# Moving the first head's key bits to ScalarE, making the bit offsets first, and fewer warm products: the start of a hash-attention and Sinkhorn-MoE kernel

## The chip, the cores and the metric

The kernel runs on one core of one Trainium2 chip. The metric is the device time of one execution in microseconds (us), as the median of several. All executions told of here were classed as fast; "clock" is the mean clock granted to TensorE, 1.0 being full. In the profiles PE is TensorE, PEld its weight loads, DVE is VectorE, ACT is ScalarE, POOL is GpSimd and SP is SyncE; a q behind an engine's name is its sequencer, which waits and issues transfers. PSUM is the memory in which this kernel has TensorE's results.

## The reference

```python
# q, k, v: (4, 8, 768, 64); proj: (64, 6)
q_bits = einsum('bhsd,dk->bhsk', q, proj) > 0      # six hash bits for each query, and so for keys
mask   = q_bucket[..., :, None] == k_bucket[..., None, :]
scores = where(mask, q @ k.T / 8, -1e9)
attn_out = softmax(scores) @ v
x = attn_out as (3072, 512)
# then: logits = x @ w_gate, 8 Sinkhorn iterations, 8 experts of relu(x @ w1[e]) @ w2[e], summed
```

## The kernel before

Eight groups of four heads go one after the other through the attention; the experts follow. A query's bits are appended as seven more rows to its 64 values, and a key's likewise, so that one product gives score and mask. `prepare(n)` makes group n ready; for group 1, VectorE transposes k and q, TensorE hashes, VectorE makes the bits (L414 to L417). Group 0 has a routine of its own, because everything waits for it:

```python
def place(name, h, c, copy):            # 32x768 float32 -> float16, all in on-chip memory
    pin(copy(d[name][32*c:32*(c+1), h, :], trs[name][32*h:32*(h+1), c, :]))

def at_once():                          # group 0
    ...
    for name in "kq":
        turn_qk(name, 0)                # VectorE transposes; GpSimd casts the result (t16)
        place(name, 0, 0, nc.scalar.copy)
        hash_twice(name, 0)             # TensorE: hash of the first two heads
        turn_qk(name, 1)
        place(name, 0, 1, nc.scalar.copy)
        ...
        warm_up(9 if name == "q" else 4)
    ...                                 # bits of k: VectorE reads PSUM, then x BIG in place
    move("k", 0)                        # two VectorE copies 7x384, the key bits of head 0
    put("k")
    ...                                 # query bits of head 0: two VectorE operations from PSUM
    ...                                 # query bits of all: one VectorE operation from PSUM
    put("q")
    place("q", 1, 1, nc.vector.tensor_copy)
    move("k", 1)                        # two copies each: bits of head 1
    move("q", 1)
    ...
    cast_v()                            # GpSimd: two casts of v, then six sums for its mean
```

For group 1, VectorE transposes k and q, TensorE hashes, VectorE makes the bits (L414 to L417) and copies those of its head 0 (L431). The bits of its other heads go to a DRAM buffer and come back:

```python
    stack("q", 0)                       # SyncE: two transfers each
    stack("q", 1)
    ...
    put_bits()                          # SyncE: ds <- bt, 96 KB to DRAM
    ...
    get_bits("k", h); get_bits("q", h)  # SyncE: back from DRAM; waits for the write
    ...
    fetch(2, "kq")                      # GpSimd: 2 x 768 KB from DRAM for group 2
```

`pin` keeps an instruction behind the one traced before it on its engine. Without it an instruction goes where the scheduler thinks it is needed.

The softmax here doesn't subtract the row's maximum and nothing guards it: scores larger than these inputs give would overflow.

Of the kernel before, what the change touches and what calls it, by code (L numbers as in the profile page):

```python
# [20 lines left out]
def kernel(  # L21
# [11 lines left out]
    nc = tc.nc  # L33
    B, H, S, D = q.shape
    assert (B, H, S, D) == (4, 8, 768, 64)
    NB = proj.shape[1]
# [10 lines left out]
    HT = S // 2  # L47
# [5 lines left out]
    R = 32  # L53
# [3 lines left out]
    KR = D + NB + 1  # L57
# [4 lines left out]
    def pin(ins):  # L62
        tc.keep_in_program_order(ins)
        return ins
# [3 lines left out]
    proj4 = consts.tile([P, 2, NB], F32)  # L68
# [302 lines left out]
    def prepare(n):  # L371

        d = grp[n] = {}
# [13 lines left out]
        def turn_qk(name, c):  # L387
            i_ap = nat[name, n][:, :, 32 * c:32 * (c + 1)]
            o_ap = trs[name][:, c, :]
            if name == "k":  # L390
                i_ap = i_ap.rearrange("p (m t) d -> p m t d", m=M4)
                o_ap = o_ap.rearrange("p (t m r) -> p m t r", t=KT, m=M4)
            else:
                o_ap = o_ap.rearrange("p (m r) -> p m r", r=R)
            pin(nc.vector.transpose(o_ap, i_ap))
            pin(nc.gpsimd.tensor_copy(t16s[name][:, c, :], trs[name][:, c, :]))

        def stack(name, h):
            for c in range(2):
                pin(nc.sync.dma_start(out=d[name][32 * c:32 * (c + 1), h, :],  # L400
                                         in_=t16s[name][32 * h:32 * (h + 1), c, :]))
# [22 lines left out]
        def get_bits(name, h):  # L424
            pin(nc.sync.dma_start(out=d[name][D:KR, h, :].rearrange("r (j t) -> r j t", j=2),
                                       in_=dss["kq"]["kq".index(name), :, h, 0:NB + 1, :].rearrange("j r t -> r j t")))
# [6 lines left out]
        def cast_v():  # L433
            v32 = wk.tile([P, 2, 3, D], F32, tag="v32", name="v32", bufs=1)
            for i in range(2):
                hs = slice(2 * i, 2 * i + 2)
                pin(nc.gpsimd.tensor_copy(va[:, hs, :, 0:D],
                                          nat["v", n][:, hs, :].rearrange("p h (t d) -> p h t d", d=D)))
            for i in range(2):
                hs = slice(2 * i, 2 * i + 2)  # L440
                pin(nc.gpsimd.tensor_tensor(v32, va[:, hs, 0:3, 0:D], va[:, hs, 3:6, 0:D], op=Alu.add))
                pin(nc.gpsimd.tensor_tensor(v32[:, :, 0], v32[:, :, 0], v32[:, :, 1], op=Alu.add))
                pin(nc.gpsimd.tensor_tensor(vs[:, hs, 0:D], v32[:, :, 0], v32[:, :, 2], op=Alu.add))

        def place(name, h, c, copy):
            pin(copy(d[name][32 * c:32 * (c + 1), h, :], trs[name][32 * h:32 * (h + 1), c, :]))

        def at_once():
            bt = wk.tile([P, 2, S], F16, tag="t16", name="bt0")

            def hash_twice(name, c):
                for g, table in enumerate((pb.rearrange("p c a r -> p c (a r)"), pb1)):
                    for x in range(2):
                        o = 64 * g + 32 * x
                        pin(nc.tensor.matmul(d["pr" + name][o:o + 32, 0, 0:HT], table[:, c, :],
                                             trs[name][:, c, x * HT:(x + 1) * HT], start=(c == 0), stop=(c == 1)))

            def move(name, h):
                for x in range(2):
                    p = 64 * h + 32 * x  # L460
                    pin(nc.vector.tensor_copy(d[name][D:KR, h, x * HT:(x + 1) * HT],
                                              bt[p:p + NB + 1, "kq".index(name), 0:HT]))

            def put(name):
                i = "kq".index(name)
                pin(nc.sync.dma_start(out=dss["kq"][i].rearrange("j h r t -> (j h r) t"), in_=bt[0:64, i, 0:HT]))

            dss["kq"] = scr.tile([2, 2, HG, 8, HT], F16, tag="ds", name="ds")
            for name in "kq":
                d["pr" + name] = sps.tile([P, 2, 512], F32, tag="s", name="pr0")  # L470
                turn_qk(name, 0)
                place(name, 0, 0, nc.scalar.copy)
                hash_twice(name, 0)
                turn_qk(name, 1)
                place(name, 0, 1, nc.scalar.copy)
                if name == "k":
                    place("k", 1, 0, nc.scalar.copy)
                else:
                    place("k", 1, 1, nc.scalar.copy)
                    place("q", 1, 0, nc.scalar.copy)  # L480
                hash_twice(name, 1)
                warm_up(9 if name == "q" else 4)
                for h in range(2, HG if name == "k" else 3):
                    stack(name, h)
            k_, q_ = bt[:, 0, 0:HT], bt[:, 1, 0:HT]
            pin(nc.vector.tensor_scalar(k_, d["prk"][:, 0, 0:HT], 0.0, 0.5, op0=Alu.is_gt, op1=Alu.subtract))
            pin(nc.vector.tensor_scalar(k_, k_, BIG, None, op0=Alu.mult))
            move("k", 0)
            put("k")
            for x in range(2):  # L490
                sl = slice(32 * x, 32 * x + NB + 1)
                pin(nc.vector.tensor_scalar(d["q"][D:KR, 0, x * HT:(x + 1) * HT], d["prq"][sl, 0, 0:HT], 0.0, qoff[sl, 0:1],
                                            op0=Alu.is_gt, op1=Alu.subtract))
            pin(nc.vector.tensor_scalar(q_, d["prq"][:, 0, 0:HT], 0.0, qoff[:, 0:1], op0=Alu.is_gt, op1=Alu.subtract))
            put("q")
            place("q", 1, 1, nc.vector.tensor_copy)
            move("k", 1)
            move("q", 1)
            stack("q", 3)
            for h in range(2, HG):  # L500
                get_bits("k", h)
                get_bits("q", h)
            cast_v()

        if n == 0:
            at_once()
            return
# [177 lines left out]
    fetch(0, "v", nc.sync)  # L685
    fetch(1, "kq", nc.sync)
    pb1 = acc_flat[:, 24 * DD - 2 * R:24 * DD].rearrange("p (c m) -> p c m", c=2)
    nc.vector.memset(pb1, 0.0)
    nc.vector.tensor_copy(pb1[R:2 * R, :, 0:NB], proj4[R:2 * R])
    warm = ops.tile([P, 512], F32, tag="o", name="warm")  # L690

    def warm_up(count):
        for _ in range(count):
            pin(nc.tensor.matmul(warm, tiny, tiny.unsqueeze(1).to_broadcast([P, 4, P]), start=True, stop=True))
# [14 lines left out]
    for u in range(len(units) + 1):  # L709
        if u < len(units):  # L710
            n, h, kt = units[u]
# [239 lines left out]
```

## Time and profile before

| | before |
|---|---|
| median of the first three runs | 766.67 us (766.44 to 767.45) |
| span of the profiled run | 765.1 us |
| TensorE, VectorE, ScalarE, GpSimd busy | 98%, 74%, 67%, 42% |
| first query transpose | 8.94 us |
| first exp, first exp of group 1 | 14.27, 33.94 us |

The first query transpose starts when q has landed from DRAM. It is the time zero of most comparisons below, called T0, because that landing differs from run to run though no edit touches the load. An exp is one ScalarE instruction of the softmax, the exponential of 128x768 scores. The first exp shows when the first scores are ready; the first exp of group 1 (exp 24, counted from 0) shows what is left of a shift when the second group starts.

### The profile page before, as it was taken

The page shows a single profiled execution, that of the slowest core. Times are in us where ns is not written, and L with a number is a line of the kernel's source. Part 1 is how long each engine was busy: PE and PEld are TensorE (multiplying, and loading weights), DVE is VectorE, ACT ScalarE, POOL GpSimd, SP SyncE. Part 2 cuts the span into 40 slices and gives each one's busy share as a digit, 9 for nine tenths or more (in the row PEclk, how much of TensorE's full clock was granted, in tenths as well). Part 3 has the DMA queues.
Part 4 walks back from the last instruction along what each step waited for, and adds up shares of the span by engine and source line. Part 5 has one row for each costly group of instructions (what it writes and reads, how often), then busy time and mean ns, then how long its engine had stood idle before and what let it go on. Part 6 is the DMA issues. An engine that isn't in the chain of part 4 may idle for free.

```text
span 765.1 us, 16738 instructions
## 1 busy us (share of the span) xinstructions
PE 747.5 (98%) x6294; PEld 517.2 (68%) x6294; DVE 567.4 (74%) x1261; ACT 514.0 (67%) x1027; POOL 318.3 (42%) x327
## 2 busy tenths in 40 slices
PE   8999999999999999999999999999999999999997
PEld 3655566566654677777777777777777777777664
DVE  6787666667579777777777777777777777777774
ACT  6986786678655777766666666666666666666661
POOL 6766353449200433443344334433543344324222
PEclk9999999999999999999999999999999999999999
DMA  8779447841030464776477648754964496443335
GB/s 227 203 195 227 126 128 174 175 124 27 2 56 8 83 108 80 125 126 115 90 130 132 112 84 144 121 95 83 171 118 90 91 165 112 84 84 83 84 77 145
DMA packets 41569, 88.08 MB, mean 115 GB/s; under 512 B 7232, under 2 KB 21840, under 8 KB 41488
## 3 DMA queue, kind: packets, MB, share of 16 engines
q0 software_dynamic: 27168, 69.49, 46.9%
q1 hardware_dynamic: 13324, 16.48, 8.2%
q10 hardware_dynamic: 996, 1.05, 0.6%
q8 instruction: 49, 0.80, 0.5%
q14 instruction: 32, 0.26, 0.1%
HBM read 53.05 MB, written 7.08 MB: 79 GB/s over the span
## 4 chain that ended last, share of the span: by engine, by line
PE 84%; DVE 6%; ACT 6%; issue 1%; DMA 1%; SPq 0%; ACTq 0%; DVEq 0%
PE a L829 18%; PE a L250 18%; PE d L829 13%; PE y L250 9%; PE st L570 6%; PE d L250 4%; ACT pt L573 4%; PE hp L647 4%; PE yp L662 3%; PE num L586 3%; PE pr L406 1%; PE hp L325 1%; PE yp L309 1%; ACT acc L241 1%; DVE hT L838 1%
## 5 line engine op out<-in xcount | busy, mean ns | idle before, releaser
L838 DVE CUSTOM_DVE_ANT_0 hT<-d,u 128x384 f16<-128x384 f32 x336 | 185.5, 553 | 96.2 <-ACT u L834 94.7
L254 ACT ACTIVATE vt<-a,p 128x256 f32<-128x256 f32 x324 | 153.3, 473 | 148.7 <-PE a L250 148.3
L834 ACT COPY u<-a 128x384 f32<-128x384 f32 x336 | 160.8, 479 | 23.5 <-PE a L829 19.9
L573 ACT ACTIVATE pt<-st 128x768 f16<-128x768 f32 x192 | 147.1, 809 | 42.5 <-PE st L570 41.8
L289 POOL DMA_DIRECT2D acc<-vt x72 | 62.0, 861 | 267.1 <-ACT vt L254 114.0
L250 PEld LDWEIGHTS <-hT 128*128 128x128 f16 x1296 | 126.3, 97 | 50.4 <-DVE hT L838 0.9
L250 PE MATMUL a<-t,hs 128*128 128x256 f16 x972 | 145.8, 273 | 2.2 <-ACT vt L254 1.0
L250 PEld LDWEIGHTS <-hs 128*128 128x128 f16 x972 | 94.8, 98 | 38.5 <-issue 2.8
L829 PEld LDWEIGHTS <-t 128*128 128x128 f16 x896 | 87.7, 98 | 36.4 <-issue 0.6
L829 PE MATMUL d<-xd,t 128*128 128x384 f16 x448 | 109.4, 326 | 0.3 <-DVE hT L838 0.3
L829 PE MATMUL a<-xT,s 128*128 128x384 f16 x448 | 109.4, 326 | 0.2
L570 PE MATMUL st<-qs,ks 71*128 71x384 f16 x384 | 94.0, 325 | 3.6 <-ACT pt L573 2.4
L250 PE MATMUL y<-t,hT 128*128 128x256 f16 x648 | 97.1, 272 | 0.0
L258 DVE SCALAR_TENSOR_TENSOR acc<-y,p,acc 128x256 f32<-128x256 f32 x162 | 77.4, 478 | 11.4 <-PE y L250 11.4
L134 POOL TENSOR_TENSOR t<-t 128x1024 f16<-128x1024 f16 (+1 forms) x39 | 81.9, 2108 | 0.1
L586 PEld LDWEIGHTS <-pt 128*128 128x128 f16 x1152 | 60.5, 97 | 25.9 <-ACT pt L573 0.4
L829 PEld LDWEIGHTS <-s 128*128 128x128 f16 x672 | 65.5, 98 | 17.5 <-issue 2.5
L586 PE MATMUL num<-va,pt 128*128 128x65 f16 x1152 | 66.5, 193 | 0.3 <-ACT pt L573 0.3
L868 ACT ACTIVATE hT<-a 128x384 f16<-128x384 f32 x112 | 54.0, 482 | 1.8 <-PE a L829 1.7
L829 PE MATMUL a<-xd,s 128*128 128x384 f16 x224 | 54.3, 323 | 0.8 <-ACT u L834 0.8
L829 PE MATMUL d<-xT,t 128*128 128x384 f16 x224 | 54.7, 326 | 0.0
L829 PE MATMUL a<-xT,t 128*128 128x384 f16 x224 | 54.7, 326 | 0.0
(121 smaller groups left out, 948.7 us busy)
## 6 DMA issues: line engine op xcount, KB each, us to landing
acc<-vt POOLq DMA_DIRECT2D x72, 512.0 KB, 4.8
t<-in_moe_w_dram POOLq DMA_DIRECT2D x26, 512.0 KB, 8.5
v<-in_v_dram POOLq DMA_DIRECT2D x28, 192.0 KB, 5.7
out_dram<-acc SPq DMA_DIRECT2D x78, 64.0 KB
acc<-in_k_dram POOLq DMA_DIRECT2D x6, 768.0 KB, 7.1
acc<-in_q_dram POOLq DMA_DIRECT2D x6, 768.0 KB, 12.2
t<-in_moe_w_dram POOLq DMA_DIRECT2D x3, 1024.0 KB, 12.0
ks<-t SPq DMA_DIRECT2D x60, 48.0 KB
```

Source lines behind the costliest of these rows:

```text
L134: pin(nc.gpsimd.tensor_tensor(o[:, sl], x[:, sl], y[:, sl], op=op))
L250: pin(nc.tensor.matmul(dst, hq[hn][:, fo, :], wq[wn][:, fo, :], start=first and fo == 0, stop=fo == FH - 1, skip_group_check=True))
L254: pin(nc.scalar.activation(out=vt[:, k], in_=a, func=Act.Copy, scale=p))
L258: pin(nc.vector.scalar_tensor_tensor(out=dst, in0=src, scalar=p, in1=dst, op0=Alu.mult, op1=Alu.add))
L289: pin(nc.gpsimd.dma_start(out=acc[:, b, i], in_=vt, accum_op=Alu.add))
L570: pin(nc.tensor.matmul(st[:, i, 0:HT], d["k"][0:KR, h, kt * P:(kt + 1) * P], d["q"][0:KR, h, i * HT:(i + 1) * HT], start=True, stop=True))
L573: pin(nc.scalar.activation(out=pt, in_=st[:, :, 0:HT], func=Act.Exp, scale=scale))
L586: pin(nc.tensor.matmul(num[:, j * (D + 1):(j + 1) * (D + 1)], pf[:, j * P:(j + 1) * P], va[:, h, kt, :], start=(kt == 0 and j == 0), stop= ...
L829: pin(nc.tensor.matmul(bk, wq[wn][:, do, f * P:(f + 1) * P], xq[xn][:, do, :], start=first and do == 0, stop=do == 1, skip_group_check=True))
L834: pin(nc.scalar.copy(t, bk))
L838: pin(add(TENSOR_ADD_SAT, out=dst, in0=bk, in1=u, s0=3e38, s1=0.0))
L868: pin(nc.scalar.activation(out=hT[:, f, hi], in_=a, func=Act.Relu))
```

## The change

Its intent is to have the first scores sooner: VectorE is relieved of two copies, the offsets of the query bits leave its busy time, and the warm products (matrix products whose result nothing reads), which fill TensorE's wait, are cut to fit. In exchange a query cast of head 1 goes from ScalarE to VectorE.

```diff
-            def move(name, h):
+            def move(name, h, copy=nc.vector.tensor_copy):
...
-                else:
-                    place("k", 1, 1, nc.scalar.copy)
-                    place("q", 1, 0, nc.scalar.copy)
...
-                warm_up(9 if name == "q" else 4)
+                warm_up(6 if name == "q" else 4)
...
-            move("k", 0)
+            move("k", 0, nc.scalar.copy)
+            place("k", 1, 1, nc.scalar.copy)
             put("k")
...
             put("q")
+            place("q", 1, 0, nc.vector.tensor_copy)
             place("q", 1, 1, nc.vector.tensor_copy)
...
-    nc.vector.memset(pb1, 0.0)
-    nc.vector.tensor_copy(pb1[R:2 * R, :, 0:NB], proj4[R:2 * R])
+    pin(nc.vector.memset(pb1, 0.0))
+    pin(nc.vector.tensor_copy(pb1[R:2 * R, :, 0:NB], proj4[R:2 * R]))
```

The last two pins make a chain: the offsets are traced before the memset, so they now must run before it.

More of the change, by code (lines that the diff above doesn't have):

```diff
@@ L456, in hash_twice @@
                                              trs[name][:, c, x * HT:(x + 1) * HT], start=(c == 0), stop=(c == 1)))
-            def move(name, h):
+            def move(name, h, copy=nc.vector.tensor_copy):
                 for x in range(2):
                     p = 64 * h + 32 * x
-                    pin(nc.vector.tensor_copy(d[name][D:KR, h, x * HT:(x + 1) * HT],
+                    pin(copy(d[name][D:KR, h, x * HT:(x + 1) * HT],
                                               bt[p:p + NB + 1, "kq".index(name), 0:HT]))
```

## The prediction

> **What bounds the kernel now.** I began with the page of the kernel before, then its chain of waits from 0 to 30 us, and then the timelines of VectorE (DVE), GpSimd (POOL), ScalarE (ACT) and TensorE (PE) around the lines that the diff touches. The page's first part:
> ```profile
> PE 747.5 (98%) x6294; PEld 517.2 (68%) x6294; DVE 567.4 (74%) x1261; ACT 514.0 (67%) x1027; POOL 318.3 (42%) x327
> ```
> TensorE is busy nearly everywhere. All that the diff edits is the preparation of the first group of heads, the first 19 us of 765.1. The change removes no product of the main stages, so it can only shift what follows the start. How far a shift travels is told by the chain of waits (start us, length us, what):
> ```profile
> 2.32 6.59 DMA acc<-in_q_dram
> ...
> 9.95 0.89 DVE acc L395
> 10.84 0.04 DVE qoff L81
> ...
> 11.74 2.05 PE warm L694 x9
> 13.79 0.45 PE st L570 x2
> ...
> 23.58 0.56 DVE bt L414
> ...
> 27.97 0.51 PE xp L613 x6
> ```
> The reader should see three things. The chain starts with the load of q, which the diff leaves alone. Nine warm products, not a data wait, stand directly ahead of the first scores. And from 23.58 to 27.92 the chain runs on VectorE alone, until it hands over to the transposes xp. VectorE's timeline over the first of these stretches (start, busy, then in brackets idle before):
> ```profile
> 11.75 0.26 DVE L487 TENSOR_SCALAR bt<-bt 128x384 f16<-128x384 f16 x1
> 12.04 0.53 DVE L461 COPY ks<-bt 7x384 f16<-7x384 f16 x2
> 12.61 1.25 DVE L492 TENSOR_SCALAR qs<-pr,qoff 7x384 f16<-7x384 f32 x2
> 13.89 0.62 DVE L494 TENSOR_SCALAR bt<-pr,qoff 128x384 f16<-128x384 f32 x1
> 14.54 1.23 DVE L446 CAST qs<-acc 32x768 f16<-32x768 f32 x1
> 15.79 0.95 DVE L461 COPY ks<-bt 7x384 f16<-7x384 f16 x2
> 16.77 1.41 DVE L461 COPY qs<-bt 7x384 f16<-7x384 f16 x2
> ```
> None of these rows has an idle time: VectorE works without a gap from 9.87 to 27.92. The next row is the four transposes of group 1 (18.21 to 21.77), then mean, nv, rn and xn, the last ending at 23.50. TensorE's second hash of group 1 (L406) ends at 23.51. So at 23.5 two strands arrive together, VectorE's own queue and TensorE's. An earlier TensorE alone gains nothing there: **the later of the two strands sets the end.** GpSimd's timeline beside it:
> ```profile
> 14.54 0.83 POOL L441 TENSOR_TENSOR v<-va 128x384 f32<-128x384 f16 x1
> 15.44 0.65 POOL L442 TENSOR_TENSOR v<-v 128x128 f32<-128x128 f32 x1
> 16.17 0.46 POOL L443 TENSOR_TENSOR vs<-v 128x128 f16<-128x128 f32 x1
> 16.71 0.83 POOL L441 TENSOR_TENSOR v<-va 128x384 f32<-128x384 f16 x1
> ```
> A 7x384 copy takes 0.25 us while GpSimd is idle (12.04 to 12.57), but 0.42, 0.51, 0.88 and 0.50 us later, and each of the slow ones ends 0.11 to 0.12 us after a GpSimd row ends (17.65 after 17.53). The cast of 14.54 ends at 15.77, 0.41 us after GpSimd's 15.36.
>
> **What the Trainium skill says.** The page "SBUF — State Buffer", section "Who interferes with whom", says that VectorE and GpSimd share a port pair as an exclusive lock, which VectorE copies, casts and tensor_scalar operations can take in their two-port modes, and that whoever issues first holds it for the whole instruction. The trace agrees: those are just the residues above, and L442, issued at 15.44 with the cast holding on to 15.77, took 0.65 us where its median over all groups is 0.454. The page "VectorE: DVE Perf Modes", section "Why PSUM operands drop a tier", excludes the two-port mode for a PSUM operand. The trace agrees: L492 and L494 read PSUM, and GpSimd's cast beside them keeps its 0.829 us. The page "TensorE: Matmul & The Clock Gate", section "What's actually happening", has the clock fall to half after about 3.4 us of idleness. In the trace the first warm products start 0.427 us apart until about 4.8 us and 0.216 apart after that; the idle 1.0 us before 7.43 did not make them slow again.
>
> **The change part by part.**
> *Bit offsets first.* L79 now precedes the memset and the copy of L688 and L689, in time that VectorE spends waiting (2.6 us for proj, 1.7 us for k). It leaves 9.84, where the chain shows it worth 0.03 us, and L81 to L83 leave 10.76 to 11.25. L486 reads a hash of k that ended by 9.05, so it starts when the last transpose issues out: about 10.80 in place of 11.16. It takes 0.55, to 11.35. **0.36 us gained on VectorE here.**
> *L487 then meets GpSimd.* It would run 11.38 to 11.64, but GpSimd's cast L396 holds 10.87 to 11.70 (10.90 now, less 0.03). In the kernel before it issued 0.02 us after that cast ended. By the residue above it ends at 11.70 + 0.11 = 11.81, giving back 0.17.
> *Key bits to ScalarE.* Two copies of 0.25 us leave VectorE. L492 needs the hash of q (ends 11.74, now 11.71) and L487, so starts near 11.84 rather than 12.61. Two of 0.61 and gaps of 0.03 end at 13.10, L494 at 13.74 (was 14.51). **VectorE is now 0.77 us ahead.** On ScalarE an ACTIVATE of 768 elements takes 0.831 and one of 384 takes 0.48 in the page, so I choose 0.5 each: its cast of q ends near 11.70, the moves run 11.86 to 12.84, and the key cast of head 1 to 13.70. The first half-scores need the first of the moves (12.36) and of L492 (12.45).
> *Fewer warm products.* Six rather than nine, at 0.216 each: 0.65 us. Six end near 12.95, so the first scores' halves run at about 12.95 and 13.13; the latter waits for L492. They end near 13.47, and exp starts when ScalarE is free, about 13.7 for 14.27. **First exp 0.57 us earlier, TensorE about 0.75.**
> *Query cast to VectorE.* A second 32x768 cast, 0.41 us once it has the port, now stands before L446 on VectorE, and ahead of the copies for head 1. Put through the lock one by one: it asks at 13.77, when GpSimd's second L437 has just issued (13.74), and waits to 14.57, ending 14.98. L441 (0.83) then holds to 15.80 and the second cast ends 16.22. L442 to 16.67, first k copy 16.78; L443 to 17.24, second 17.35; L441 to 18.18, first q copy 18.30; L442 to 18.75, second q copy 18.87. Before, that was 18.18. So the gain of 0.77 becomes a **loss of 0.69 us on VectorE**: each copy pays for one more GpSimd instruction.
> *Where it lands.* Head 1's first scores (TensorE at 18.32 before, its second half near 18.48) need that last copy. With TensorE 0.75 ahead it would reach them near 17.7 and wait 1.2 us, to 18.92: 0.45 late. VectorE's xn ends at 23.50 + 0.69 = 24.19, TensorE's hash at 23.96; the later one sets L414: 24.23 for 23.58. **Sum: 0.65 us later,** and nothing in the chain from 28 to 80 us (exp, scores, transposes, hashes) is anchored to an unchanged DMA, so I expect it to reach the end. I take 0.45 of it as the central value, since the lock races below can only turn out kinder: 766.67 + 0.45, rounded to **767.1 us**.
>
> **The rivals.**
> *A: the lead survives.* If the copies for head 1 were not late, TensorE would gain 0.65 to 0.75 us throughout: 766.0. For it: the warm products really stand on the chain, and the intent of the diff is plain. Against it: the tie at 23.5, and VectorE's lack of a gap up to there. Without the port lock VectorE would gain 0.77 - 0.45 = 0.3 us: 766.3.
> *B: the cast wins the port one step earlier.* If it asks before 13.74, it runs 13.80 to 14.21 between the two L437, and the same working ends at 18.47: VectorE 0.29 late, the whole 0.25: 766.9. It is a matter of some 0.03 us, and my 0.5 for ScalarE doesn't touch it.
> *C: a cold clock.* Fewer warm products and a wait of 1.2 us before head 1 could halve the clock. Against it: TensorE's row in the page's slices has no digit under 8, and an idle 1.0 us did no harm earlier. If it happened, 3 to 5 us at half speed: 769 or more.
> *D: nothing moves,* because another wait between 28 and 70 us has slack: 766.7.
>
> **Range and chances.** Rival A gives the low end, 766.0, and my own working plus half a microsecond of the spread (766.44 to 767.45 for one kernel) the high end, 768.2. 2% is 15.3 us; none of these comes near it, and only an unseen reordering or a cold clock that lasted could. So 0.985 for within 2%, 0.005 faster, 0.01 slower.
>
> **What would show it.** Right: no qoff row after 5 us; L486 near 10.8 and L487 stretched beyond 0.3 us; six warm products and the first scores near 13.0; first exp near 13.6; two L446 rows on VectorE that each take over 0.7 us; the last q copy of head 1 after 18.4; a TensorE wait of about 1 us before head 1's first scores; L414 after 23.8 and xp after 28.1. Wrong: casts of 0.4 us, the last copy before 18.0, and L414 ahead of 23.3, when rival A holds. If these rows are all as I say and the end is still not later, the step that fails is that the shift travels.

## The result, and the profile after

The changed kernel took 767.19 us (766.63 to 767.79, six runs), the kernel before 766.81 us (766.44 to 768.04, six runs). A ratio here is the one for the fast runs of the two kernels; it is not quite the ratio of the two medians. It is 1.0003, with a 95% interval of 0.999 to 1.0015: the same.

The page of the changed kernel, first part and granted clock:

```profile
PE 746.6 (97%) x6291; PEld 516.7 (67%) x6291; DVE 567.3 (74%) x1260; ACT 514.8 (67%) x1028; POOL 319.3 (42%) x327
...
PEclk9999999999999999999999999999999999999999
```

Three products, one VectorE instruction less and one ScalarE instruction more: two copies moved over, one cast back. The granted clock is a 9 (90% or more) in every slice, with a mean of 0.999. The chain of waits of the changed kernel (start us, length us, what), from 0 to 30 us:

```profile
2.32 7.08 DMA acc<-in_q_dram
...
9.42 1.84 DVE acc L395 x2
11.26 0.45 DVE bt L483
...
14.23 1.18 DVE qs L446
...
15.42 1.09 DVE qs L446
...
18.42 0.51 DVE qs L461
...
18.95 3.56 DVE acc L395 x4
...
26.59 7.38 DMA ds<-bt
```

q landed 0.48 us later than in the trace before, by chance as the later runs show. The warm products have left the chain. VectorE's queue has taken their place, up to the transposes of group 1 and beyond, and behind it stands something that the chain before didn't have: the bits of group 1 on their way through DRAM. VectorE's timeline of the changed kernel:

```profile
11.73 0.53 DVE L484 TENSOR_SCALAR bt<-bt 128x384 f16<-128x384 f16 x1
12.29 1.25 DVE L490 TENSOR_SCALAR qs<-pr,qoff 7x384 f16<-7x384 f32 x2
13.58 0.62 DVE L492 TENSOR_SCALAR bt<-pr,qoff 128x384 f16<-128x384 f32 x1
14.23 2.28 DVE L446 CAST qs<-acc 32x768 f16<-32x768 f32 x2
16.54 0.94 DVE L461 COPY ks<-bt 7x384 f16<-7x384 f16 x2
17.51 1.42 DVE L461 COPY qs<-bt 7x384 f16<-7x384 f16 x2
18.95 0.98 DVE L395 STREAM_TRANSPOSE acc<-acc 128x768 f32<-128x768 f32 x1
```

No row has an idle time before it. L492 starts 4.16 us after T0, where L494 before started at 4.96: VectorE is 0.8 us ahead. The transposes of group 1 start 9.54 us after T0, for 9.28 before: now it is 0.26 us behind. In between stand two query casts for one, at over a microsecond each. TensorE at head 1's first scores, and what ended its idle time:

```profile
18.44 0.34 PE L569 MATMUL st<-qs,ks 71*128 71x384 f16 x1 [0.32 <-DVE qs L461]
18.98 0.32 PE L569 MATMUL st<-qs,ks 71*128 71x384 f16 x1 [0.20 <-DVE qs L461]
```

Both halves wait for VectorE's copies. The second half of the first scores had come at T0 + 4.18 (before 4.98), but the second half of head 1's comes at T0 + 9.56 (before 9.54): the lead of 0.80 is gone. From there on, times after T0:

| | before | changed |
|---|---|---|
| first exp | 5.34 | 4.80 |
| exp 6 (head 1) | 9.96 | 9.98 |
| bits of group 1 (L414) | 14.64 | 14.74 |
| exp 24 | 25.01 | 24.92 |
| exp 30 (head 1 of group 1) | 29.44 | 30.17 |
| exp 48 | 45.77 | 45.96 |

### The profile page after: what moved, and what is told of

The parts are those of the page before. It is cut to its first block, busy times and chain, and to the rows that moved or that the text cites. A ratio compares the mean times of both kernels' runs of the same rounds, so it can differ in the third digit from the quotient of the medians.

```text
span 766.1 us, 16731 instructions
## 1 busy us (share of the span) xinstructions
PE 746.6 (97%) x6291; PEld 516.7 (67%) x6291; DVE 567.3 (74%) x1260; ACT 514.8 (67%) x1028; POOL 319.3 (42%) x327
## 4 chain that ended last, share of the span: by engine, by line
PE 83%; DVE 7%; ACT 6%; DMA 2%; issue 1%; SPq 0%; ACTq 0%; DVEq 0%
PE a L828 18%; PE a L250 18%; PE d L828 13%; PE y L250 9%; PE st L569 5%; PE d L250 4%; PE hp L646 4%; PE yp L661 3%; ACT pt L572 3%; PE num L585 3%; PE hp L325 1%; PE yp L309 1%; ACT acc L241 1%; PE pr L406 1%; DVE hT L837 1%
```

## The experiments

Every run was correct. Theory T says that VectorE's lead is lost to the port that it shares with GpSimd, and that a shift of the start is carried to the end. Its rivals, lettered as in the prediction, say that the lead survives (A), that fewer warm products bring a slow clock (C), or that some other wait takes any shift back (D); some runs name one more of their own. The kernel before ran beside them.

### The changed kernel again

No edit.

> The changed kernel once more, for its spread. Theory T (VectorE's lead is lost to the port it shares with GpSimd, and the shift is then carried to the end): between 0.0 and +0.6 us against the kernel before, and the trace repeats the order of the changed kernel's: group 1's transposes 0.2 to 0.4 us later than before when both are counted from the start of the first query transpose (before 9.28, changed 9.54), two query casts on VectorE of over 1 us each, a wait of TensorE of about 0.8 us before head 1's first scores. Rival A (a gain of the start, hidden by chance): -0.3 us or less. The query load's landing, 8.94 us before and 9.42 in the changed kernel, is taken for chance: here anywhere from 8.8 to 9.6.

Measured: 766.43 us against 766.36, ratio 1.0001 (0.9987 to 1.0014). T0 was 8.85, the group's transposes came at T0 + 9.31, the casts took 0.97 and 1.08 us, exp 6 came at T0 + 9.75 and exp 24 at T0 + 24.69. The order repeats, but three expectations failed: the transposes are 0.03 us later than before and not 0.2 to 0.4, one cast is just under 1 us, and TensorE waited 0.2 us before head 1's first scores and not 0.8. (That 0.8 was too much for the first trace as well: 0.32 and 0.20 us.) v had landed 0.21 us sooner after T0 than in the first trace of this kernel, which a table below takes up. The change costs nothing that these rounds can see. The 0.38 us between the medians of the first comparison became 0.07 here.

### Offsets first, alone

```diff
-    nc.vector.memset(pb1, 0.0)
+    pin(nc.vector.memset(pb1, 0.0))        # and the copy of the next line likewise
```

> The kernel before with only the bit offsets made first. Counted from the start of the first query transpose: L486 at 1.76 us for 2.23; L487 stretched to over 0.4 us because GpSimd's cast holds the port; then Theory T has the one query cast of VectorE win the port one GpSimd instruction sooner, so that group 1's transposes start at 8.9 for 9.28. The end does not follow, because TensorE's strand (nine warm products) is unchanged: group 1's bits (L414) 0.0 to 0.15 us earlier, the end within 0.2 us. Rival (the offsets are worth what they leave the queue): everything 0.36 us earlier, the end too.

Measured: 766.57 us against 766.36, ratio 1.0001 (0.9987 to 1.0014). L486 at T0 + 1.76, L487 stretched to 0.53 us, transposes of group 1 at T0 + 8.93, L414 at 14.46. The numbers are close to what was expected (L414 0.18 us earlier, where 0.15 was the most allowed), but not for the reason given: v had landed sooner than in the trace before, and the transposes stand 5.24 us after GpSimd's first v cast in both. The offsets gave VectorE nothing that lasted.

### Six warm products, alone

```diff
-                warm_up(9 if name == "q" else 4)
+                warm_up(6 if name == "q" else 4)
```

> The kernel before with six warm products in place of nine. Theory T: the second half of the first scores waits for VectorE's query bits, which end just 0.05 us before it starts, so first exp, group 1's transposes and the end stay where they are, within 0.1 us in the trace when counted from the first query transpose. Rival (the chain of waits shows the warm products on the path, so they cost what they last): first exp 0.65 us earlier, and up to 0.65 us of it at the end. Rival C (clock falls): warm products or scores 0.4 us apart, end some us later.

Measured: first exp at T0 + 5.34, exp 6 at T0 + 9.96, both just as before. So the warm products were on the chain only because VectorE's bits ended 0.05 us ahead of them; cutting them alone gains nothing. But the time was 768.17 us, ratio 1.0024 (1.001 to 1.0038), two runs of four above 769 with a clock of 0.997. The chain of waits of this trace from 24 to 50 us:

```profile
25.58 8.80 DMA ds<-bt
...
38.04 7.37 DMA ks<-ds
...
45.77 0.77 PE st L570 x2
```

and the busy time of each engine, granted clock and transfers from 42 to 46 and 46 to 50 us (PE, PEld, DVE, ACT, POOL, clock, share of the transfer engines, GB/s):

```profile
42.00:46.00 4.00, 1.88 (x24) 1.03 (x21) 2.76 (x8) 2.25 (x3) 1.08 (x2) 0.98 1.06 192
46.00:50.00 4.00, 4.00 (x31) 2.44 (x30) 1.97 (x5) 1.95 (x3) 0.13 (x1) 0.59 1.11 263
```

The bits of group 1 took 8.8 us to DRAM, the later fetch of head 2's key bits 7.4 us, TensorE waited 1.9 us for them, and the clock fell to half at 45.84 us and came back at 49.25. The span grew by 2.8 us. Rival C had a fall of the clock, but no theory had it come from a transfer some 30 us later, so the run was repeated:

> The kernel with six warm products and nothing else of the change, again. Its first run was 0.24% slower, two of four runs at 769.2 to 769.6; in its trace the scores of group 1's head 3 waited 1.9 us for key bits to come back from DRAM, at 43.9 us, and the granted clock fell to half for 3.4 us after that. Theory T (chance of the transfers, not the six products, which are 20 us past): the median within 0.6 us of before, at most one run in five or six over 768.5. Rival C (six products bring the fall of the clock): again about half of the runs over 769.

Measured: 767.86 us against 766.84, ratio 1.0012 (0.999 to 1.0034), two of six runs above 771 with a clock of 0.995, one at 768.1. The head that waits is head 2 of group 1, counted from 0; the text on record says 3. In this trace TensorE waited 2.6 us and the clock was at half for 6.8 us. With six products five of ten runs were above 768 us, against three of the forty executions of the kernel before. Chance at that rate is not an easy answer, and rival C is not either: the changed kernel has the same six products and had no run above 768 in eleven.

### The exchange, alone

```diff
-            move("k", 0)
+            move("k", 0, nc.scalar.copy)       # and both place() calls that the change moves
```

> The kernel before with only the exchange: key bits of the first head on ScalarE, the query cast of head 1 on VectorE; offsets and nine warm products as before. Theory T: VectorE pays one more GpSimd instruction: two query casts of about 1 us, group 1's transposes at 9.5 to 9.7 us after the first query transpose (before 9.28), group 1's bits 0.2 to 0.3 us later, the end 0.1 to 0.4 us later. First exp about 0.1 us earlier only. Rival (the exchange is balanced: two copies of 0.25 away, one cast of 0.41 added, and L492 sooner): transposes at 8.9 to 9.2, end no later.

Measured: 766.22 us against 766.36, ratio 1.0 (0.9986 to 1.0014). First exp at T0 + 5.22. The casts took 0.72 and 1.08 us, and group 1's transposes came at T0 + 9.29, 5.54 us after the v cast. The 0.3 us that a second cast costs are there when counted from the v cast, but v had landed 0.29 us sooner after T0 than in the trace before, and that hid them: L414 came at 14.53 (before 14.64) and the end no later. From T0, the expectation failed on the first cast, the transposes, L414 and the end; that the v cast is the right zero was read off the traces only now. Later runs put it to the test.

By now a rule for this kernel stood out. Here it is with all fourteen traces, seven of them from runs that are told of below (us; the first number is from the start of the span, those of the v cast, the transposes and exp 24 are after T0):

| kernel | T0 | v cast | group 1's transposes | transposes less v cast | exp 24 |
|---|---|---|---|---|---|
| before | 8.94 | 4.04 | 9.28 | 5.24 | 25.01 |
| before, again | 8.76 | 3.84 | 9.09 | 5.24 | 25.03 |
| offsets alone | 9.09 | 3.69 | 8.93 | 5.24 | 24.87 |
| six warm alone | 8.54 | 3.71 | 8.95 | 5.24 | 24.89 |
| six warm alone, again | 9.14 | 3.89 | 9.13 | 5.24 | 24.82 |
| bits written first | 8.61 | 3.93 | 9.17 | 5.24 | 25.11 |
| six warm, bits first | 8.60 | 3.85 | 9.09 | 5.24 | 25.04 |
| changed | 9.42 | 3.98 | 9.54 | 5.55 | 24.92 |
| changed, again | 8.85 | 3.77 | 9.31 | 5.54 | 24.69 |
| exchange alone | 8.49 | 3.75 | 9.29 | 5.54 | 24.68 |
| 3 us late | 9.25 | 3.60 | 9.14 | 5.54 | 26.85 |
| GpSimd held back | 8.60 | 3.81 | 7.09 | 3.29 | 26.43 |
| casts on GpSimd | 8.73 | 4.53 | 7.63 | 3.10 | 24.30 |
| casts on GpSimd, bits first | 8.95 | 4.53 | 7.63 | 3.10 | 24.31 |

With one query cast on VectorE it is 5.24, with two 5.54 to 5.55, whatever VectorE did before. In these eleven traces it doesn't matter how early VectorE comes to its copies; it leaves in step with GpSimd's chain of v casts and sums, and the start of that chain is set by the landing of v. The landings themselves scatter by more than the change could move: T0 from 8.49 to 9.42.

### GpSimd held back

```diff
+   # after the first of the two v casts: GpSimd reads what VectorE's last copy writes
+   pin(nc.gpsimd.tensor_copy(gate_[D:KR, :], held))      # held = d["q"][D:KR, 1, S-2:S]
```

> The changed kernel in which GpSimd, after its first v cast, has to wait for VectorE's last query bits of head 1 (a copy of two elements that reads them), so that the six copies meet an idle GpSimd. Theory T: the two query casts take 0.41 to 0.45 us each for 1.18 and 1.08, the four copies 0.25 each for 0.40 to 0.88, group 1's transposes start near 6.8 us after the first query transpose for 9.54. In exchange GpSimd's sums are late and the mean of head 0 waits for them, so no gain at the end is expected: within 0.6 us. Rival (the copies are slow of themselves: 32 or 7 partitions, or a partition shift): the casts stay over 0.9 us.

Measured: VectorE's timeline,

```profile
13.41 1.11 DVE L449 CAST qs<-acc 32x768 f16<-32x768 f32 x2
14.56 0.54 DVE L464 COPY ks<-bt 7x384 f16<-7x384 f16 x2
15.12 0.54 DVE L464 COPY qs<-bt 7x384 f16<-7x384 f16 x2
15.70 1.84 DVE L395 STREAM_TRANSPOSE acc<-acc 128x768 f32<-128x768 f32 x2
```

0.55 us for each cast and 0.25 to 0.26 for each copy. The same six instructions took 4.69 us in the changed kernel (14.23 to 18.92) and take 2.25 here. They are slow because of GpSimd, not of themselves; the rival falls. The expected 0.41 for a cast was too low: that was the residue after a wait; so the transposes came at T0 + 7.09 and not near 6.8. The end was a miss: 769.9 us against 766.84, ratio 1.0032 (1.0016 to 1.0048), where 0.6 us had been allowed. Who waited for whom from 17 to 26 us tells why:

```profile
PE mp L598 <- POOL vs L446: 2.0, 1, 2.0
```

TensorE stood 2.0 us for GpSimd's last sum. GpSimd's chain of sums can't be put off by 3 us, so this is a test and not a remedy. The trace is of the fastest of the four runs (768.29 us); the other three, at 769.6 to 770.3 with clocks of 0.997 and 0.998, lost more than it shows, and where is open.

### The query casts on GpSimd

GpSimd has 1.25 us of idle time before v lands. Both casts are traced there, ahead of the v casts. They take 1.68 us, so the v casts start somewhat late, at T0 + 4.53:

```diff
+                else:
+                    place("q", 1, 0, nc.gpsimd.tensor_copy)
+                    place("q", 1, 1, nc.gpsimd.tensor_copy)
...
-            place("q", 1, 0, nc.vector.tensor_copy)
-            place("q", 1, 1, nc.vector.tensor_copy)
```

> The changed kernel with both query casts of head 1 moved from VectorE to GpSimd, into the 1.25 us in which GpSimd waits for v. Theory T (VectorE is slaved to GpSimd's chain by the shared port, 5.24 us from GpSimd's first v cast to group 1's transposes with one query cast on VectorE, 5.54 to 5.56 with two, whatever else the four kernels differ in): with none, the copies of head 1 find one or two GpSimd instructions fewer ahead of them: transposes at 7.3 to 8.2 us after the first query transpose (before 9.28, changed 9.54), no wait of TensorE before head 1's first scores, exp 6 at 9.2 (9.96), group 1's bits 0.5 to 0.75 us earlier than before. The end 0.3 to 0.7 us earlier if that travels, none of it if a transfer between 30 and 46 us sets the pace. Rival (ScalarE and TensorE set the pace, not the port): no change of exp 6 against the changed kernel.

Measured: GpSimd's and then VectorE's timeline,

```profile
11.52 1.68 POOL L446 CAST qs<-acc 32x768 f16<-32x768 f32 x2
13.27 1.62 POOL L437 CAST va<-v 128x768 f16<-128x768 f32 x2
...
13.54 1.46 DVE L461 COPY ks<-bt 7x384 f16<-7x384 f16 x2
15.03 1.30 DVE L461 COPY qs<-bt 7x384 f16<-7x384 f16 x2
16.36 0.98 DVE L395 STREAM_TRANSPOSE acc<-acc 128x768 f32<-128x768 f32 x1
```

Transposes at T0 + 7.63, exp 6 at T0 + 9.16, no wait of TensorE before head 1's first scores, L414 at T0 + 13.91: all within what Theory T had put down. exp 24 is 0.71 us ahead of before and exp 48 0.50. The time was 766.42 us against 766.84, ratio 0.9998 (0.9981 to 1.0015), one run of six at 769.76 with a clock of 0.996: a gain at the end is not resolved. The rival falls: exp 6 came 0.82 us sooner than in the changed kernel. The transposes came 1.91 us sooner, which is more than the 1.10 us of two casts that meet no GpSimd work, so the rest was waiting for GpSimd. The port is still not free: the four copies took 2.8 us here and 1.1 with GpSimd held back.

### Three microseconds late

```diff
-                warm_up(6 if name == "q" else 4)
+                warm_up(20 if name == "q" else 4)
```

> The changed kernel with 20 warm products instead of 6 ahead of the first scores: 14 x 0.216 = 3.0 us of TensorE's time. Does a shift of the start travel to the end? Theory T (it travels whole): first exp 3.0 us later less the 0.57 that had waited for ScalarE, so 2.3 to 2.6; the wait before head 1's first scores is gone, so from exp 6 on 2.1 to 2.3 us; end 2.0 to 2.4 us later than before. Rival D (a transfer between 28 and 46 us has slack or sets the pace): the shift at exp 24 is 2.2 and at exp 48 under 1.5, and the end with it.

Measured: first exp at T0 + 7.53 (2.2 us later than before, just under the 2.3 expected), exp 6 2.20, exp 24 1.84 (2.1 expected) and exp 48 2.05 us later, time 769.21 us against 766.84, ratio 1.0027 (1.0012 to 1.0042), a difference of 2.4 us in the medians. A late start is carried whole to the end. Rival D falls for delays.

### The order in which the bits are written

The traces offered a cause for the long waits after "six warm alone". SyncE writes the bits of group 1 (ds) only after eight transfers of 0.5 to 0.6 us of issue time each; GpSimd issues the big loads of group 2 in its own time. How the write stood to the key load, and how long it was before SyncE could fetch the first bits back (us):

| kernel | write issued after the key load | until the first fetch is issued |
|---|---|---|
| GpSimd held back | -0.54 | 4.5 |
| changed, again | -0.16 | 7.0 |
| before; changed; exchange alone | 0.07; 0.07; 0.08 | 7.5; 7.4; 7.4 |
| offsets alone | 0.30 | 7.9 |
| six warm alone, again | 0.45 | 9.2 |
| casts on GpSimd | 0.53 | 8.4 |
| six warm alone | 0.53 | 8.8 |
| 3 us late | 1.66 | 7.9 |

The later the write, the longer the wait, though not strictly (9.2 at 0.45, then 8.4 and 8.8), and the last line does not fit; there the loads were further along when the write was issued, but that this is the reason was not tested. Theory Q takes the order for the cause. (Its text swaps the pair of "six warm": it was 9.2 us at 0.45 and 8.8 at 0.53.) The test is one step of order, in group 1 only:

```diff
         stack("q", 0)
-        stack("q", 1)
...
         put_bits()
+        stack("q", 1)
```

> Six warm products in the kernel before, plus one step of order: in group 1 SyncE issues the write of the hash bits to DRAM ahead of the two transfers of head 1's queries, not behind them. Theory Q (the wait of 1.9 and 2.6 us before head 2 of group 1, and the fall of the clock after it, come from a race of queues: the later the bits are written after GpSimd has issued the 768 KB key load of group 2, the longer they take; 0.45 and 0.54 us behind it they took 8.8 and 9.2 us, 0.07 behind it 7.5, 0.54 ahead of it 4.5): the write is issued 0.0 to 0.4 us ahead of that load, the bits are back at 21.5 to 24 us after the first query transpose for 25.9 and 26.4, no wait over 0.5 us on TensorE between 28 and 50 us, no run above 768.5, median 766 to 767. Rival C (six products make the clock fall in some other way): half of the runs above 768 again.

> The kernel before with that order of SyncE alone. Theory Q: the bits are back 0.5 to 3 us sooner than the 24.5 of the kernel before, but nothing waited for them there, so the trace's scores stay where they are and the median is within 0.4 us of before; its rare slow runs (769.64 in eleven, 768.04 in six) go. Rival (the transfers between 26 and 46 us pace the kernel before as well): 0.5 us or more faster.

Measured with six warm products: 766.59 us (766.18 to 766.96) against 766.83, ratio 0.9994 (0.9982 to 1.0007), no run above 767, no wait of TensorE over 0.5 us between 25 and 52 us. SyncE's timeline of this trace,

```profile
24.76 0.35 SPq L422 DMA_DIRECT2D ds<-bt  x1
...
29.51 0.27 SPq L425 DMA_DIRECT2D ks<-ds  x1
```

beside that of the kernel before:

```profile
25.90 0.53 SPq L422 DMA_DIRECT2D ds<-bt  x1
...
33.40 0.27 SPq L425 DMA_DIRECT2D ks<-ds  x1
```

The write now goes 0.49 us ahead of the key load (0.4 at most had been expected) and the first fetch follows after 4.8 us, not 7.5 (and 8.8 to 9.2 without the step). At T0 + 20.9 the bits are back sooner than the expected 21.5. The step does two things at once: it puts the write ahead of GpSimd's load, and it takes two transfers of 48 KB from ahead of it in SyncE's own queue. That the shorter queue does it is a rival that no run was made for, but the packets of the kept traces speak against it. With nine products the write's 128 packets of 768 bytes begin 2.7 us after its issue with the step and 2.9 without; they are through in 0.9 us with it and in 3.9 without, and in that time GpSimd's queue moved 116 and 1,200 KB. And in "GpSimd held back", with SyncE's old order but the load late, they are through in 0.9 us too.

With nine warm products and the same step: 766.40 us, ratio 0.9994 (0.9981 to 1.0006), bits back at T0 + 20.8, exp 24 unchanged (0.1 us later); as expected, nothing had waited there in the trace before. The 0.43 us between the medians lies between what the theory and its rival had allowed, and inside the interval. That the rare slow runs go can't be told: the nine runs of the kernel before beside it had none above 768 either.

> The kernel before, unchanged, as a run of its own: what chance alone makes of time and trace. The first v cast of GpSimd, 4.04 us after the first query transpose in the first trace, lies between 3.6 and 4.0 here; group 1's transposes then come 5.24 us after that cast (Theory T) and so at 8.85 to 9.25; the end within 0.5 us; at most one run in six above 768.5 with a clock mean of 0.998 or less. If half of the runs of this kernel were slow too, six warm products would have nothing to do with it.

Measured: 767.01 us (766.64 to 768.73) against 766.83, ratio 1.0006 (0.9993 to 1.002). v cast, transposes and the rule of 5.24 as expected. One thing counts against a simple form of Theory Q: here too the write came late, 0.46 us behind the key load, and took 8.3 us, yet TensorE did not wait. The kept traces tell why: there is a second race. The fetch of head 2's key bits comes after the late write in SyncE's queue, and it meets the key load of group 3. In the two traces with the long wait it was issued 0.55 and 0.87 us behind that load, and landed 7.4 us after; here it went 0.77 us ahead of it and landed in 1.8. In none of the other twelve traces was it behind, and in none did TensorE wait for it. So the kernel before runs near an edge, about 0.8 us from it in this trace. That the order of the queues makes the round trip long is shown by three kernels with the step, each against its like without it. That it also makes the slow runs is likely, not proven: with six products none of five runs was above 768 us with the step and five of ten without it, which chance alone would give about once in twelve. Why six products alone fall over the edge more often than nine stays open.

### Both remedies together

Both casts on GpSimd in the changed kernel, and the bits written first.

> Both query casts of head 1 on GpSimd in the changed kernel, and that order of SyncE: the version meant to beat both kernels. Theories T and Q together: group 1's transposes at 7.3 to 8 us, exp 24 about 0.7 us earlier than before (24.3 for 25.0), and, since the bits come back well before head 1 of group 1 wants them, the 0.7 still there at exp 48; end 0.4 to 0.8 us earlier than before, 766.0 where before has 766.7, ratio 0.9990 to 0.9996, and no run above 768. Rival D (some other wait takes the lead back by 50 us): exp 48 within 0.3 us of before.

Measured: 766.25 us (765.76 to 766.83) against 766.83, ratio 0.9991 (0.9979 to 1.0004). Transposes at T0 + 7.63, exp 24 0.70 us ahead of before, exp 48 0.39, no run above 767. It is 0.6 us below the kernel before, as the two theories had it, but the interval includes 1: five rounds don't prove a gain of this size. Part of the lead of exp 24 is gone by exp 48, between the expectation of theories T and Q and that of rival D.

## Why the prediction was right, point by point

- **What bounds the kernel, and the tie of two strands.** Right in the main. Earlier scores alone bring nothing, as the first exp of the changed kernel shows (0.54 us earlier, all lost by exp 6). Predicted for it: 0.57. Two slips of reading changed nothing: TensorE's row of slices does have a digit under 8, the last, a 7; and 0.831 us is ScalarE's cast of 32x768, not its ACTIVATE of 128x768 (0.809).
- **Offsets first.** Right: L79 to L83 ran from 1.21 to 1.93 us, and the bits of k started 0.47 us sooner after T0 (predicted 0.36).
- **L487 meets GpSimd.** Right: 0.53 us in place of 0.26, ending 0.11 after GpSimd's cast. The lock that the prediction took from the skill was borne out here and by the held-back run.
- **ScalarE's copies.** 0.51 us each, estimated as 0.5. VectorE was 0.80 us ahead at the query bits, predicted 0.77.
- **The query cast at the port.** The mechanism was right and its size was off. This is the mis-sized term: a loss of 0.69 us on VectorE was predicted, 0.26 was measured after T0 and 0.31 after the v cast. The working let a GpSimd instruction that waits behind a cast take its full time after it, though the prediction had the counter-example in hand: its L442, blocked to 15.77, ended at 16.09. GpSimd's rows of the changed kernel,

```profile
14.97 1.13 POOL L441 TENSOR_TENSOR v<-va 128x384 f32<-128x384 f16 x1
16.17 0.65 POOL L442 TENSOR_TENSOR v<-v 128x128 f32<-128x128 f32 x1
```

  end 0.68 and 0.32 us after the cast that blocked each (15.41 and 16.51), where the two take 0.83 and 0.45 alone. That is 0.28 of the 0.38 to 0.43 that the term was too large.
- **Where it lands.** Head 1's scores were to wait 1.2 us and waited 0.32 and 0.20; they were to come 0.45 late and came 0.02 late; L414 was to be 0.65 late and was 0.10 late (0.12 early in the second trace). So the sum was too high: at exp 24 the changed kernel is 0.1 to 0.3 us ahead, not 0.65 behind.
- **That a shift is carried to the end.** Right for a delay of the start (3 us late: 2.4 us); for a gain no run resolved it. Wrong in its reason: "nothing in the chain from 28 to 80 us is anchored to an unchanged DMA" overlooked the round trip of the bits. In the first trace of the changed kernel TensorE waited 0.53 us, to 39.01, ahead of head 1 of group 1. The profile names the move of its queries (qs<-t) for TensorE and its query bits (qs<-ds) for the weight load; the landings decide for the bits: the queries had landed by 30.5 us, the query bits, issued at 34.31, at 38.81. Exp 30 came 0.73 late after T0, of which 0.2 was left at exp 48. Of the 1.0 us by which that trace's span is longer, 0.48 is its T0, 0.2 this, and 0.3 came after the last exp (203 us) and was not followed up.
- **The time.** 767.1 was predicted and 767.19 measured, and the range held it. The closeness is partly luck: with the second set the change of the medians is 0.07 us rather than 0.38. What the runs support is no gain and no loss within 0.15%. Of the rivals, B's size of loss on VectorE (0.29) is nearest, though not by its route: the cast did not win the port one step earlier. D, "nothing moves", describes the time best.

## What to carry to other kernels

Before work is moved onto an engine, look at what that engine meets at the new place. Here six copies and casts in on-chip memory took VectorE 4.69 us beside a busy GpSimd and 2.25 beside an idle one, while an operation that read PSUM kept its 0.61. Time gained ahead of that stretch was lost in it, because VectorE left it in step with GpSimd; moving two of the casts to GpSimd brought group 1 forward by 0.7 us, though no gain at the end was resolved. And where a small round trip through DRAM shares the queues with large loads, try to issue it ahead of them: 0.6 us in their order took three off the round trip here (7.5 to 4.6).

## What the Trainium skill lacked or had wrong

- "SBUF — State Buffer", section "Who interferes with whom", says that the loser of the shared port pair fully blocks. It does not say that part of the blocked instruction's time passes during the block (the page has a figure for the time after the release, about 115 ns, only for a DMA whose descriptors GpSimd writes): GpSimd's sums ended 0.68 and 0.32 us after the release where they take 0.83 and 0.45 alone; VectorE's copies ended 0.11 after it where they take 0.25, its cast 0.41 where it takes 0.55. It is about 0.14 us each time.
  The section also says that issue order decides; the runs agree, and show it for a VectorE instruction that asks in the middle of a GpSimd instruction: it asked at 14.23, the next GpSimd instruction's row begins at 14.97, and VectorE was served at 15.00 when the first ended.
- "DMA: Bandwidth & Descriptors" tells how queues share the transfer engines packet by packet, but no figure was found in it for what that does to a small transfer: the first fetch behind a 96 KB write to DRAM could be issued after 4.5 to 4.9 us when the write went 0.5 to 0.75 us ahead of two 768 KB loads, and after 7.4 to 9.2 us when it went 0.07 to 0.53 us behind the first of them. The write's packets took 0.9 to 1.5 us in the first case and 3.1 to 4.8 in the second.
- "TensorE: Matmul & The Clock Gate", section "What's actually happening", gives the fall of the clock after a window of about 3.4 us of idleness, and does not say how much work a window may hold and still count as idle; the page's section on a second failure mode tells of falls from frequent short idle times, without their lengths. Here it fell after an unbroken wait of only 1.9 us (at 45.84 us; TensorE was busy 1.9 of the 4 us from 42 to 46) and in another run 1.5 us into a wait of 2.6. It stayed at half for 3.4 and for 6.8 us, one and two such windows.
